# Attention scores in seven runs of three and two key blocks instead of eight of two, beside an MLP on one Trainium2 core

## The chip, the cores and the metric

The kernel runs on one core of one Trainium2 chip. Times are microseconds of the device for one execution. Before the change three runs gave a median of 1385.5 us (1382.28 to 1387.74). The core has a matrix engine (PE, with PEld for its weight loads), a vector engine (DVE), a scalar engine for activations (ACT), a general engine (POOL), and an engine that issues DMAs (SP). PE writes its results to PSUM, a small memory that DVE and ACT read; everything else lies in SBUF or in DRAM.

## The reference

For an input x of 2048 tokens by 640, with 32 heads of 20:

```python
xn = _layernorm(x, axis=-1)
# attention on xn
q, k, v = split(xn @ wqkv)                    # 32 heads of 20
scores = einsum("bhqd,bhkd->bhqk", q, k) * (Dh ** -0.5)
p = _softmax(scores, axis=-1)
A = merge(einsum("bhqk,bhkd->bhqd", p, v)) @ wo
# MLP on the normed xn, normed again
h = _gelu(_layernorm(xn) @ w1 + b1)           # 640 -> 1536
B = h @ w2 + b2                               # 1536 -> 640
return x + A + B
```

All is float32. The kernel computes the matrix products from pairs of float16 (a high and a low part) in three passes, and the product of exponentials and values partly in that way and partly in float32.

## The kernel before, in words

**Ahead of attention** (to about 232 us) the input is normed, transposed and projected to q, k and v. q, k and the normed input go to DRAM (`qkscr`, `xscr`), the factor of the second norm to `rscr`, and v stays in SBUF as `vfull`, with a column of ones a head.

**The attention stage** takes the heads in 16 pairs `g` and the queries in two halves `hf` of 1024, in the order `ORDER` (line 37). For each (g, hf) `load_stack` (line 131) brings a `qs` and a `ks`, each holding both heads of the pair with three stacked copies of 20 rows and a row for the shift, 61 rows a head. Each half has two columns of 512 queries, `cc`. For each of these 64 (g, hf, cc) there are 16 blocks `kb` of 128 keys; the texts call them a sixteen.

One block: `scores` (line 578) takes a buffer `s` of PSUM (pool `psS`, three buffers, line 53) and a buffer `p` of SBUF (pool `pt`, 2 * GRP - 1 = 7 buffers, line 517), issues two matmuls, one for each head (line 584, on the upper and the lower half of the PE's rows), and has ACT write the exponential to `p` (line 586). For blocks 0 and 1 of each four (`SPLIT`, line 25) `rest` (line 593) has DVE make `low`, what is left of `p` beyond its upper 16 bits (line 598; four buffers). `pv` (line 603) issues the products with the values for four blocks at once: eight matmuls with the upper halves, four with the `low`s, and for the two unsplit blocks four in float32, which show as eight records, all at line 615, into one PSUM buffer `o` (`psO`, one buffer). After a sixteen's last products ACT copies `o` to `ev` (line 636). `ev` holds both columns, and after the second one `unload` (line 644) issues six DMAs to `lpart` and `opart`, on SP, or on ACT for the last pair (`dma`, line 640). When a unit of heads is complete, `finish` (line 666) reads these back, divides and writes `oscr`.

**The MLP** is a generator, `mlp` (line 829), that yields the estimated cost of each step it has issued: 0.3276 for three matmuls of layer 1 (line 787), 0.272 for two of layer 2 (line 819). It takes 256 tokens a round, eight rounds. In layer 1 a unit is 30 matmuls into the one buffer of `psM`, and its last step begins `gelu` (line 735): DVE work at once, more at the next `tick`, tanh on ACT (line 748) two ticks later, the rest one tick later. In layer 2 a unit is 36 matmuls for 320 columns of 128 tokens, with `addup` behind it. Six units of layer 1 and four of layer 2 alternate in a round. `load_chunk` (line 769) loads a round's input `xm` and its factors `r2f` two rounds ahead. After the MLP `projection` (line 872) multiplies `oscr` with wo (line 896) and writes the output; it runs almost wholly behind attention.

**The order of the work** is written out by hand under `tc.manual_schedule()` (lines 927 to 983): each engine works through its instructions in the order in which they are issued here, and waits for semaphores. Before the change a group of four blocks is: two blocks' scores, a `tick` (which moves every open generator in `sides` one step), `rest` of the first, an MLP part; two more blocks' scores, a `tick`, `rest` of the others, and `pv` of the four blocks before. A part takes steps from the generator while `credit` is above zero, less than `CHUNK` has been spent, and no unit has ended (`over`); credit grows by `rate` at each part and is kept.

Of the kernel before, what the change touches and what calls it, by code (L numbers as in the profile page):

```python
# [7 lines left out]
F32 = mybir.dt.float32  # L8
# [8 lines left out]
P = 128  # L17
# [25 lines left out]
def mha_mlp_kernel(tc, x, wqkv, wo, w1, b1, w2, b2, out):  # L43
# [4 lines left out]
    with (  # L48
# [463 lines left out]
        with ExitStack() as scope:  # L512
# [1 line left out]
            m0 = pool(name="m0", bufs=2)  # L514
            m1 = pool(name="m1", bufs=1)
            m2 = pool(name="m2", bufs=2)
            ptp = pool(name="pt", bufs=2 * GRP - 1)


            sides = []  # L520
# [77 lines left out]
                    nc.vector.tensor_sub(low, pt, upper(pt))  # L598
                    unit.append(low)

            evs = {}

            def pv(units):

                g, hf, cc, kb0 = units[0][:4]
                if kb0 == 0:
                    pv.o = psO.tile([P, 512], F32, tag="o", name="o")  # L610
                    pv.begun = set()
                last = units[-1][3] == NKB - 1

                def product(q, src, v0, t):
                    nc.tensor.matmul(pv.o[32 * q : 32 * q + 32, :], src[:, v0 - PAD * (1 - q % 2) :][:, :32], t,  # L615
                                     start=q not in pv.begun, stop=last, skip_group_check=True)
                    pv.begun.add(q)

                split = [(u[3], upper(u[4]), u[5]) for u in units if SPLIT[u[3]]]
                whole = [(u[3], u[4]) for u in units if not SPLIT[u[3]]]  # L620
                of16 = lambda kb, a: 2 * PAD + kb * 2 * VROW + (2 * g + a) * 2 * VW
                of32 = lambda kb, a: PAD + kb * VROW + (2 * g + a) * VW
                for kb, up, _ in split:
                    for a in range(2):
                        product(2 * a, vhalf, of16(kb, a), up[:, a])
                        product(2 * a + 1, vhalf, of16(kb, a) + VW, up[:, a])
                for a in range(2):
                    for n, (kb, _, low) in enumerate(split):
                        product(2 * a + n % 2, vhalf, of16(kb, a), low[:, a])
                for a in range(2):  # L630
                    for n, (kb, pt) in enumerate(whole):
                        product(2 * a + n % 2, vfull, of32(kb, a), pt[:, a])
                if last:
                    if cc == 0:
                        evs[g, hf] = m1.tile([P, 2, 512], F32, tag="ev", name="ev")
                    nc.scalar.activation(evs[g, hf][:, cc], pv.o, AF.Copy)  # L636
                    if cc == 1:
                        unload(g, hf, evs.pop((g, hf)))

            def dma(g, hf):  # L640

                return (nc.scalar if (g, hf) == ORDER[-1] else nc.sync).dma_start

            def unload(g, hf, ev):
                cols = slice(hf * 1024, (hf + 1) * 1024)
                for p in range(2):
                    dma(g, hf)(lpart[p, hf, 2 * g : 2 * g + 2, :].rearrange("a (c t) -> a c t", c=2),
                                      ev[PAD + DH + VW * p :: 64])
                    for a in range(2):
                        q0, r = 64 * a + PAD + VW * p, (2 * g + a) * DH  # L650
                        dma(g, hf)(opart[p, r : r + DH, cols].rearrange("d (c t) -> d c t", c=2),
                                          ev[q0 : q0 + DH])
# [82 lines left out]
            def gelu(ps, r2f, hT, f):  # L735
                u = m1.tile([P, 2, MC], F32, tag="u", name="u")
                w = m1.tile([P, 2, MC], F32, tag="w", name="w")
                if f == 0:
                    nc.vector.tensor_scalar(r2f, r2f, f1, None, ALU.mult)
                nc.vector.tensor_mul(u, ps, r2f[:, None, :].to_broadcast([P, 2, MC]))  # L740
                nc.vector.tensor_add(u, u, b1t[:, f : f + 2, None].to_broadcast([P, 2, MC]))  # L741
                yield

                nc.vector.tensor_mul(w, u, u)  # L744
                nc.vector.scalar_tensor_tensor(w, w, 1.0 / 0.044715, u, ALU.add, ALU.mult)  # L745
                yield
                yield
                nc.scalar.activation(w, w, AF.Tanh, scale=0.7978845608028654 * 0.044715)
# [14 lines left out]

            NMC = S // MC

            xs, hTs = {}, {}
            over = [False]

            def load_chunk(mc):
                t0 = mc * MC  # L770
                xnt = m2.tile([P, KD, 2, MC], F16, tag="xnt", name="xm")
                r2f = m2.tile([P, MC], F32, tag="r2f", name="r2f")
                nc.sync.dma_start(xnt, xscr[:, :, :, t0 : t0 + MC])
                nc.sync.dma_start(r2f, rscr[None, t0 : t0 + MC].to_broadcast([P, MC]))
                xs[mc] = xnt, r2f

            def layer1(mc, f):
                xnt, r2f = xs[mc]
                if f == 0:
                    hTs[mc] = m0.tile([P, KF, 2, MC], F16, tag="hT", name="hT")  # L780
                ps = psM.tile([P, 2, MC], F32, tag="m", name="pu")
                for i in range(2):
                    n = 0
                    fo_ = (f + i) % 4 * P
                    for k in range(KD):
                        for a, b in PASS:
                            nc.tensor.matmul(ps[:, i], w1v[:, k, (f + i) // 4, a, fo_ : fo_ + P], xnt[:, k, b, :],  # L787
                                             start=(n == 0), stop=(n == 3 * KD - 1))
                            n += 1
                            if n % 3 == 0:  # L790
                                if i == 1 and n == 15:
                                    begin(gelu(ps, r2f, hTs[mc], f))
# [35 lines left out]

            def mlp():
                load_chunk(0)  # L830
                load_chunk(1)
                yield 2.0
                for mc in range(NMC + 1):
# [93 lines left out]
            with tc.manual_schedule():  # L927
                fill = chain()
                credit = 0.0 - next(fill)
                rate = 1.235  # L930
                groups = [(g, hf, cc, kb) for g, hf in ORDER for cc in range(2) for kb in range(0, NKB, GRP)]
                prev = None
                for g, hf, cc, kb0 in groups:
                    units = []
                    for kb in range(kb0, kb0 + GRP):
                        units.append([g, hf, cc, kb, scores(g, hf, cc, kb)])
                        if kb % 2 == 0:
                            continue
                        tick()
                        if kb % GRP == 1:  # L940

                            rest(units[0])
                            credit += rate
                            spent, over[0] = 0.0, False
                            while credit > 0 and spent < CHUNK and not over[0]:
                                cost = next(fill)
                                if cost is None:
                                    credit = 0.0  # L950
                                    break
                                credit -= cost
                                spent += cost
                        else:
                            for u in units[1:]:
                                rest(u)
                            if prev:
                                pv(prev)
                    prev = units
                    if cc == 0 and kb0 == 0 and (g, hf) != ORDER[-1]:  # L960
                        n = ORDER[ORDER.index((g, hf)) + 1]
                        sides.append(load_stack(*n, *([stacks[g, hf][1]] if n[0] == g else [])))
                n = 0
                ended[0] = True

# [9 lines left out]
                    return True  # L975

                more(2)
                pv(prev)
                while more(1):
                    pass  # L980
                while sides:
# [101 lines left out]
```

## Time and profile before

| | |
|---|---|
| median of three runs | 1385.5 us |
| the profiled execution's own time | 1385.2 us |
| its span | 1383.5 us |
| granted PE clock, mean | 0.997 |
| PE, DVE, ACT busy | 1350.8, 1061.7, 1126.2 us |
| first exponential of attention begins | 233.18 us |
| last products of attention begin | 1307.89 us |

A page row of a group names line, engine, operation, tiles and shapes and a count, then busy time and the mean of one in ns, then the idle time of the engine just before these instructions and what ended most of it. Rows in order of time begin with the start and the duration in us; a bracket names idle time before the first of them. Matmuls are pipelined and their ends are modelled, so the distance between two starts tells more than a duration.

### The profile page before, as it was taken

What the parts mean: (1) busy time and instruction counts of PE and PEld (TensorE: products, weight loads), DVE (VectorE), ACT (ScalarE), POOL (GpSimd) and SP (SyncE); (2) the same over time, 40 slices, a digit from 0 to 9 for tenths busy, and PEclk for the clock granted to TensorE, in tenths of its full rate; (3) what the DMA queues carried; (4) which work ended last, traced back from release to release, by engine and by line L of the source; (5) the groups of instructions that cost most, each with busy time, mean ns of one, the idle gap of its engine ahead of it and who ended that gap; (6) DMA issues with size and microseconds to landing.
All of it is one profiled execution on the core that took longest, in us unless ns stands there. A gap on an engine that the chain in (4) does not pass through costs nothing.

```text
span 1383.5 us, 29113 instructions
## 1 busy us (share of the span) xinstructions
PE 1350.8 (98%) x11711; PEld 600.9 (43%) x11711; DVE 1061.7 (77%) x1425; ACT 1126.2 (81%) x1282; POOL 32.9 (2%) x75
## 2 busy tenths in 40 slices
PE   9999999999999999999999999999999999999998
PEld 6555555443333343433343333343334334333375
DVE  6648743899778977889887789877988897888642
ACT  5644323999999999999999999999999999999700
POOL 2000000000000000000000000000000000000000
PEclk9999999999999999999999999999999999999999
DMA  9853413012124231213221123212124322341375
GB/s 265 243 175 109 108 52 110 16 32 64 41 55 111 67 88 34 69 52 102 71 77 33 47 75 103 76 47 58 44 64 113 98 56 70 85 153 59 98 235 179
DMA packets 92320, 125.68 MB, mean 91 GB/s; under 512 B 16905, under 2 KB 58569, under 8 KB 92178
## 3 DMA queue, kind: packets, MB, share of 16 engines
q1 hardware_dynamic: 89218, 117.14, 28.3%
q0 software_dynamic: 2304, 5.24, 2.3%
q8 instruction: 94, 1.54, 0.5%
q10 hardware_dynamic: 656, 1.36, 0.3%
q14 instruction: 48, 0.39, 0.1%
HBM read 80.84 MB, written 42.86 MB: 89 GB/s over the span
## 4 chain that ended last, share of the span: by engine, by line
PE 59%; DVE 11%; ACT 5%; DMA 3%; issue 2%; SPq 1%; DVEq 0%; ACTq 0%
PE o L615 23%; PE s L584 14%; PE py L819 9%; PE pu L787 8%; DVE low L598 5%; PE z L896 5%; ACT p L586 4%; DMA oscr<-oa 1%; DVE u L740 1%; DMA oa<-opart 1%; DVE u L741 1%; DVE w L744 1%; DVE w L745 1%; DVE hT L752 1%; DVE u L750 1%
## 5 line engine op out<-in xcount | busy, mean ns | idle before, releaser
L586 ACT ACTIVATE p<-s 128x1024 f32<-128x1024 f32 x1024 | 973.6, 1042 | 52.4 <-PE s L584 46.2
L598 DVE TENSOR_TENSOR low<-p 128x1024 f16<-128x1024 f32 x512 | 608.8, 1219 | 165.0 <-ACT p L586 164.9
L615 PE MATMUL o<-p,vfull 128*32 128x512 bf16 (+1 forms) x4096 | 433.7, 494 | 0.0
L584 PE MATMUL s<-qs,ks 61*128 61x512 f16 x2048 | 317.7, 382 | 8.7 <-ACT p L586 7.2
L584 PEld LDWEIGHTS <-ks 61*128 61x128 f16 x2048 | 63.9, 94 | 296.4 <-issue 294.2
L787 PE MATMUL pu<-xm,w1t 128*128 128x256 f16 x1440 | 179.2, 274 | 4.1 <-DVE u L740 3.6
L819 PE MATMUL py<-w2t,hT 128*128 128x320 f16 x1152 | 178.6, 301 | 1.7 <-DVE xb L757 1.7
L787 PEld LDWEIGHTS <-w1t 128*128 128x128 f16 x1440 | 130.9, 98 | 71.2 <-issue 57.6
L819 PEld LDWEIGHTS <-hT 128*128 128x128 f16 x1152 | 102.5, 98 | 89.5 <-issue 55.2
L286 PE MATMUL qkp<-xnt,wv 128*128 128x512 f16 x600 | 132.3, 380 | 0.0
L615 PEld LDWEIGHTS <-vfull 128*32 128x32 f16 x3072 | 61.5, 95 | 146.2 <-issue 115.4
L615 PE MATMUL o<-low,vfull 128*32 128x512 f16 x1024 | 107.3, 379 | 6.6 <-DVE low L598 6.4
L300 ACT ACTIVATE qkhl<-qkp,qks 128x1024 f16<-128x1024 f32 (+1 forms) x24 | 23.3, 971 | 84.1 <-PE qkp L286 66.2
L286 PEld LDWEIGHTS <-wv 128*128 128x128 f16 x600 | 58.2, 98 | 67.8
L615 PEld LDWEIGHTS o<-p,vfull 128*32 128x32 f32 x2048 | 63.1, 109 | 50.6 <-issue 0.5
L349 PE MATMUL vp<-wv,xnt 128*128 128x320 f16 x480 | 66.6, 300 | 0.0
L896 PE MATMUL z<-w1t,ot 128*128 128x320 f16 x480 | 65.8, 300 | 0.0
L896 PEld LDWEIGHTS <-ot 128*128 128x128 f16 x480 | 46.7, 98 | 19.8 <-issue 1.7
L349 PEld LDWEIGHTS <-xnt 128*128 128x128 f16 x480 | 46.5, 98 | 18.2
L301 DVE SCALAR_TENSOR_TENSOR qkhl<-qkp,qks,qkhl 128x1024 f16<-128x1024 f32 (+1 forms) x24 | 26.5, 1104 | 34.3 <-ACT qkhl L300 34.3
L857 DVE SCALAR_TENSOR_TENSOR acc<-z,sc,acc 128x320 f32<-128x320 f32 x32 | 17.6, 550 | 45.1 <-PE z L896 42.9
L636 ACT ACTIVATE ev<-o 128x512 f32<-128x512 f32 x64 | 39.4, 615 | 3.3 <-PE o L615 3.3
(168 smaller groups left out, 685.7 us busy)
## 6 DMA issues: line engine op xcount, KB each, us to landing
qkscr<-qkhl SPq DMA_DIRECT2D x40, 256.0 KB
opart<-ev SPq DMA_DIRECT2D x124, 80.0 KB
ks<-qkscr SPq DMA_DIRECT2D x120, 80.0 KB
qs<-qkscr SPq DMA_DIRECT2D x192, 40.0 KB
oa<-opart SPq DMA_DIRECT2D x32, 240.0 KB
xt<-in_A_x_dram SPq DMA_DIRECT2D x16, 320.0 KB
xscr<-xnt SPq DMA_DIRECT2D x4, 1280.0 KB
xm<-xscr SPq DMA_DIRECT2D x8, 640.0 KB
```

Source lines behind the costliest of these rows:

```text
L286: nc.tensor.matmul(ps[:, i, :], wv[:, k, q, a, mm * P : (mm + 1) * P], xnts[c][:, k, b, :], start=(k + n == 0), stop=(k == KD - 1 and n == 2))
L300: nc.scalar.activation(hl[:, 0, i0:i1], ps[:, i0:i1], AF.Copy, scale=a)
L301: nc.vector.scalar_tensor_tensor(hl[:, 1, i0:i1], ps[:, i0:i1], a, hl[:, 0, i0:i1], ALU.mult, ALU.subtract)
L349: nc.tensor.matmul(ps[:, hf, :320], xnts[c][:, k, a, j * P : (j + 1) * P], wv[:, k, 2, b, hf * 320 : (hf + 1) * 320], start=(n == 0), stop ...
L584: nc.tensor.matmul(ps[:, a, :], ks[64 * a : 64 * a + 61, kb * P : (kb + 1) * P], qs[64 * a : 64 * a + 61, cc * 512 : (cc + 1) * 512], star ...
L586: nc.scalar.activation(pt, ps, AF.Exp, scale=QS)
L598: nc.vector.tensor_sub(low, pt, upper(pt))
L615: nc.tensor.matmul(pv.o[32 * q : 32 * q + 32, :], src[:, v0 - PAD * (1 - q % 2) :][:, :32], t, start=q not in pv.begun, stop=last, skip_gr ...
L636: nc.scalar.activation(evs[g, hf][:, cc], pv.o, AF.Copy)
L787: nc.tensor.matmul(ps[:, i], w1v[:, k, (f + i) // 4, a, fo_ : fo_ + P], xnt[:, k, b, :], start=(n == 0), stop=(n == 3 * KD - 1))
L819: nc.tensor.matmul(ps[:, :320], hTs[mc][:, f, a, j * P : (j + 1) * P], w2v[:, f, b, hf * 320 : (hf + 1) * 320], start=(n == 0), stop=(n == ...
L896: nc.tensor.matmul(ps[:, :320], ot[:, k, a, j * P : (j + 1) * P], wov[:, k, b, h * 320 : (h + 1) * 320], start=(n == 0), stop=(n == 3 * KD ...
```

## The change

- The order: a sixteen's scores go in seven runs, ending after blocks 3, 5, 7, 9, 12, 14 and 16 (so 3, 2, 2, 2, 3, 2, 2 blocks). Behind the runs stand, in this order: an MLP part, the products of the last four blocks of the sixteen before, an MLP part, the products of blocks 0 to 3, those of 4 to 7, an MLP part, those of 8 to 11. `rest` follows each run for all its blocks. There are seven ticks for eight.
- MLP parts: three for four; `rate` 1.647 for 1.235, `CHUNK` 2.0 for 1.75.
- Buffers: eight of exponentials for seven. `ev` holds one column, and is unloaded after each. `r2f` has one buffer for two and is loaded by itself, one round ahead, where the last unit of layer 1 has begun its GELU.
- `gelu` has one tick fewer ahead of tanh.

```diff
-CHUNK = 1.75
+CHUNK = 2.0
...
-            ptp = pool(name="pt", bufs=2 * GRP - 1)
+            ptp = pool(name="pt", bufs=2 * GRP)
...
                 if last:
-                    if cc == 0:
-                        evs[g, hf] = m1.tile([P, 2, 512], F32, tag="ev", name="ev")
-                    nc.scalar.activation(evs[g, hf][:, cc], pv.o, AF.Copy)
-                    if cc == 1:
-                        unload(g, hf, evs.pop((g, hf)))
+                    ev = m1.tile([P, 512], F32, tag="ev", name="ev")
+                    nc.scalar.activation(ev, pv.o, AF.Copy)
+                    unload(g, hf, cc, ev)
...
-            def unload(g, hf, ev):
-                cols = slice(hf * 1024, (hf + 1) * 1024)
+            def unload(g, hf, cc, ev):
+                c0 = cc * 512
                 for p in range(2):
-                    dma(g, hf)(lpart[p, hf, 2 * g : 2 * g + 2, :].rearrange("a (c t) -> a c t", c=2),
-                                      ev[PAD + DH + VW * p :: 64])
+                    dma(g, hf)(lpart[p, hf, 2 * g : 2 * g + 2, c0 : c0 + 512], ev[PAD + DH + VW * p :: 64])
                     for a in range(2):
                         q0, r = 64 * a + PAD + VW * p, (2 * g + a) * DH
-                        dma(g, hf)(opart[p, r : r + DH, cols].rearrange("d (c t) -> d c t", c=2),
-                                          ev[q0 : q0 + DH])
-                if g + 1 in ENDS:
+                        dma(g, hf)(opart[p, r : r + DH, hf * 1024 + c0 : hf * 1024 + c0 + 512], ev[q0 : q0 + DH])
+                if cc == 1 and g + 1 in ENDS:
...
                 yield
-                yield
                 nc.scalar.activation(w, w, AF.Tanh, scale=0.7978845608028654 * 0.044715)
...
+            def load_factors(mc):
+                r2f = m1.tile([P, MC], F32, tag="r2f", name="r2f")
+                nc.sync.dma_start(r2f, rscr[None, mc * MC : (mc + 1) * MC].to_broadcast([P, MC]))
+                fs[mc] = r2f
...
                 if f == KF - 2:
+                    if mc + 1 < NMC:
+                        load_factors(mc + 1)
                     if mc + 2 < NMC:
                         load_chunk(mc + 2)
...
-                rate = 1.235
-                groups = [(g, hf, cc, kb) for g, hf in ORDER for cc in range(2) for kb in range(0, NKB, GRP)]
...
+                rate = 1.647
+                after = {3: "mlp", 5: -GRP, 7: "mlp", 9: 0, 12: GRP, 14: "mlp", 16: 2 * GRP}
+                prev, units, new = None, [], []
+                for g, hf in ORDER:
+                    for cc in range(2):
+                        prev, units = units, []
+                        for kb in range(NKB):
+                            units.append([g, hf, cc, kb, scores(g, hf, cc, kb)])
+                            new.append(units[-1])
+                            work = after.get(kb + 1)
+                            if work is None:
+                                continue
+                            tick()
+                            for u in new:
                                 rest(u)
+                            new.clear()
+                            if work == "mlp":
...
+                            elif work >= 0:
+                                pv(units[work : work + GRP])
+                                units[work : work + GRP] = [None] * GRP
+                            elif prev:
+                                pv(prev[work:])
+                                prev = None
+                                del u
...
                 more(2)
-                pv(prev)
+                pv(units[-GRP:])
```

More of the change, by code (lines that the diff above doesn't have):

```diff
@@ new lines, in mha_mlp_kernel @@
+                rate = 1.647
[12 more added lines that the diff above has]
+                            for u in new:
+                                rest(u)
+                            new.clear()
+                            if work == "mlp":
+                                credit += rate
+                                spent, over[0] = 0.0, False
+                                while credit > 0 and spent < CHUNK and not over[0]:
+                                    cost = next(fill)
+                                    if cost is None:
+                                        credit = 0.0
+                                        break
+                                    credit -= cost
+                                    spent += cost
+                            elif work >= 0:
[5 more added lines that the diff above has]
+                                del u
+                            if cc == 0 and work == -GRP and (g, hf) != ORDER[-1]:
+                                n = ORDER[ORDER.index((g, hf)) + 1]
+                                sides.append(load_stack(*n, *([stacks[g, hf][1]] if n[0] == g else [])))
```

39 lines of the change are left out of this document (5 added, 34 removed).

## The prediction

> **What bounds the kernel now.** I read the page first, then the groups by line, then the waits, then the order of time of a few stretches, because the change moves instructions within one stage.
>
> ```profile
> span 1383.5 us, 29113 instructions
> PE 1350.8 (98%) x11711; PEld 600.9 (43%) x11711; DVE 1061.7 (77%) x1425; ACT 1126.2 (81%) x1282; POOL 32.9 (2%) x75
> PE   9999999999999999999999999999999999999998
> ACT  5644323999999999999999999999999999999700
> L586 ACT ACTIVATE p<-s 128x1024 f32<-128x1024 f32 x1024 | 973.6, 1042 | 52.4 <-PE s L584 46.2
> L584 PE MATMUL s<-qs,ks 61*128 61x512 f16 x2048 | 317.7, 382 | 8.7 <-ACT p L586 7.2
> PE s L584 <- ACT p L586: 7.2, 24, 0.5
> PE o L615 <- DVE low L598: 6.4, 11, 1.5
> 700.00:800.00 100.00, 98.75 (x931) 39.21 (x929) 80.72 (x88) 96.38 (x109) 0.87 (x1) 1.00 0.18 45
> ```
>
> The slices show two nearly full engines from slice 8 to slice 37: that is the attention stage, and in the window 700 to 800 PE is busy 98.75 us and ACT 96.38 us, at a granted clock of 1.00. ACT's idle time before the exponentials (52.4 us) waits on PE's scores. PE itself waits little: 7.2 us in 24 waits for an exponential, 6.4 us in 11 waits for a `low`. So PE's stream of instructions sets the time, with ACT close behind. The time to sum against is the profiled execution's 1385.2 us (its span is 1383.5); the median of the three runs is 1385.5, so both bases are the same within 0.3 us.
>
> **The prices.** One stretch of the order of time gives them all, as distances between starts on PE and on ACT.
>
> ```profile
> 702.22 1.16 PE L787 MATMUL pu<-xm,w1t 128*128 128x256 f16 x9
> 703.31 0.61 PE L584 MATMUL s<-qs,ks 61*128 61x512 f16 x4
> 703.84 0.64 PE L615 MATMUL o<-p,vfull 128*32 128x512 bf16 x8
> 705.49 0.61 PE L584 MATMUL s<-qs,ks 61*128 61x512 f16 x4
> 705.77 0.63 ACT L636 ACTIVATE ev<-o 128x512 f32<-128x512 f32 x1
> 706.03 1.81 PE L787 MATMUL pu<-xm,w1t 128*128 128x256 f16 x15
> 706.25 3.96 ACT L586 ACTIVATE p<-s 128x1024 f32<-128x1024 f32 x4
> 707.78 0.61 PE L584 MATMUL s<-qs,ks 61*128 61x512 f16 x4
> 710.09 0.63 ACT L748 ACTIVATE w<-w 128x512 f32<-128x512 f32 x1
> 710.61 9.52 ACT L586 ACTIVATE p<-s 128x1024 f32<-128x1024 f32 x10
> ...
> 727.15 1.25 PE L819 MATMUL py<-w2t,hT 128*128 128x320 f16 x8
> 728.33 0.61 PE L584 MATMUL s<-qs,ks 61*128 61x512 f16 x4
> 731.65 0.61 PE L584 MATMUL s<-qs,ks 61*128 61x512 f16 x4
> 732.08 4.00 ACT L586 ACTIVATE p<-s 128x1024 f32<-128x1024 f32 x4 [0.64 <-PE s L584]
> 732.19 1.53 PE L819 MATMUL py<-w2t,hT 128*128 128x320 f16 x10
> 733.65 0.60 PE L584 MATMUL s<-qs,ks 61*128 61x512 f16 x4
> ```
>
> ```profile
> 233.18 7.44 ACT L586 ACTIVATE p<-s 128x1024 f32<-128x1024 f32 x8
> 234.25 0.39 PE L584 MATMUL s<-qs,ks 61*128 61x512 f16 x2 [0.52 <-ACT p L586]
> 272.73 0.39 PE L584 MATMUL s<-qs,ks 61*128 61x512 f16 x2 [0.19 <-ACT p L586]
> 273.05 0.66 PE L615 MATMUL o<-p,vfull 128*32 128x512 bf16 x8
> ...
> 349.78 1.03 ACT L586 ACTIVATE p<-s 128x1024 f32<-128x1024 f32 x1 [0.38 <-PE s L584]
> ```
>
> ```profile
> L748 ACT ACTIVATE w<-w 128x512 f32<-128x512 f32 x48 | 30.6, 637 | 0.0
> ```
>
> A run of two blocks (four matmuls) takes 703.84 - 703.31 = 0.53, and one block that began alone behind a wait 273.05 - 272.73 = 0.32. So a block is **0.21** and every run carries **0.11** on top. Four blocks of products are 705.49 - 703.84 = **1.65**. An MLP part of 9 matmuls is 1.09 and one of 15 is 1.75: **0.11 a matmul and 0.11 a part**; in layer 2, 8 take 1.18 and 10 take 1.46, or 0.135 each and 0.12 a part. On ACT, eight exponentials run in 7.44, one alone shows 1.03, so they follow each other by (7.44 - 1.03) / 7 = **0.915**; `ev` delays the next by 0.48, tanh by 0.52. An exponential starts **0.45** behind the start of its block (732.08 - 731.65 = 0.43, rounded up for others at 0.49). A score buffer is free for PE **1.07** after its exponential began (234.25 - 233.18).
>
> For 16 blocks of keys, PE needs 8 x 0.53 + 4 x 1.65 + 4.94 of MLP (the rate, 4 x 1.235) + 4 x 0.11 = 16.2, ACT 16 x 0.915 + 0.48 + 0.75 x 0.52 = 15.5 (48 tanh, L748's row, on 64 sixteens). ACT has 0.7 to spare on the average, and only three score buffers to carry it over PE's other work.
>
> **What goes.** Seven runs for eight and three parts for four: two pieces fewer in each of 64 sixteens, 2 x 0.11 x 64 = **-13.9 us**. Products and MLP matmuls are as many as before.
>
> [...]
>
> The waits of the products for a `low` go too. They came because block 1's `low` (of each four) was issued on DVE behind a whole MLP part's GELU work, with its products one run away. Now the `low`s of a run follow that run, and their products stand four blocks or more later. A record's end is modelled 0.38 after its start while starts lie 0.21 apart, so each recorded wait hides another 0.17: 6.4 + 11 x 0.17 = **-8.3 us** (bounds: 0, if as many remain, and -8.3).
>
> **What comes: waits for score buffers.** Block n writes the buffer of block n-3, so it waits for that exponential. Before, with runs of two and X between them, the second block reuses the first block's buffer of the last run: free at 0.45 + 1.07 = 1.52 from that run's start, reached at 0.53 + X + 0.21. X may be as short as 0.78; products (1.65) leave 0.87 to spare. With a run of three this changes:
> - Two, products, three: the third block needs the second's buffer, free at 0.45 + 0.915 + 1.07 = 2.43, reached at 0.53 + 1.65 + 0.42 = 2.60. Spare: 0.17, for blocks 2 and 11 of each 16.
> - Three, X, two: again 2.43, reached at 0.74 + X + 0.21. X must be 1.48: products leave 0.17, an MLP part of 9 matmuls (1.09) is 0.39 short, one of 4 (0.66) is 0.82 short.
>
> Any backlog on ACT adds: `ev`, tanh, a score left over. And the parts get unequal. A part ends at 2.0 us of credit or at a unit's end; layer 1's unit (30 matmuls) falls into 21 + 9 and layer 2's (36) into 16 + 16 + 4, as the built order shows, where before most parts were 8 to 12. ACT starves behind the long ones (2.4 and 2.3 us) and PE stands behind the short ones.
>
> I carried these prices through the built order of both kernels, block by block (PE in its order; a block not before 1.07 after the start of exponential n-3; ACT in its order). From first to last block before comes to 1048.0 with 16.1 of such waits. The trace has 1304.78 - 232.47 = 1072.3 there:
>
> ```profile
> 232.47 0.61 PE L584 MATMUL s<-qs,ks 61*128 61x512 f16 x4
> 1304.78 0.61 PE L584 MATMUL s<-qs,ks 61*128 61x512 f16 x4
> ```
>
> The rest is waits for DVE and DMA, which I left out, and a slower start. After comes to 1059.0 with 44.3 of waits (block 4: 12.3, block 2: 10.6, block 11: 7.5, block 15: 7.4), and 3.5 us of matmuls (20 of layer 2, 6 of the projection) now stand behind the last score, moved and not added. The waits grow by **+28.2 us**. Bounds: before, the trace records 24 waits, 7.2 + 24 x 0.17 = 11.3, where the same walk has 15.3 in waits longer than 0.17; scaled by that 0.74 the growth is +20.9. With 0.943 between exponentials, (9.52 - 1.03) / 9 from the row of ten at 710.61, in which short waits are merged, the walk gives +35. I take 28, the plain price.
>
> **Unloading and the rest.** `ev` is unloaded after each half, so 192 more DMA issues, all but the last pair's on SP, at about half a microsecond by the rows below. SP waits for ACT there (370.6 us in 22 waits), so it is early; what stands behind a waiting unload are loads of stacks needed eight or more blocks later: nothing. `ev` has one buffer, written every 16 us, and its six issues take 3.2 us (below), so it is free long before: nothing. For the last pair the issues are ACT's own, and the new set comes in the middle of its exponentials:
>
> ```profile
> SPq L647 <- ACT ev L636: 370.6, 22, 29.9
> 1310.31 1.08 ACTq L647 DMA_DIRECT2D lpart<-ev  x1
> 1311.42 0.72 ACTq L651 DMA_DIRECT2D opart<-ev  x2
> 1312.17 0.50 ACTq L647 DMA_DIRECT2D lpart<-ev  x1
> 1312.71 0.86 ACTq L651 DMA_DIRECT2D opart<-ev  x2
> ```
>
> That is 1.08 + 0.72 + 0.50 + 0.86 = 3.2 us in which PE runs out of score buffers; less the spare in them, **+2 us** (bounds 0 and 3.2).
>
> The eighth buffer of exponentials keeps the old rule (the ninth block's exponential needs a buffer whose first products follow its score at once), GELU's missing step brings tanh one run earlier (L748 waits 0.0 us now), and r2f's load comes two parts ahead of its use. Each costs nothing while ACT's 0.7 us a sixteen covers it; a tanh late by 0.7 in half of 48 cases would be 17 us of ACT, most of it in that slack.
>
> **Sum:** 1385.2 - 13.9 - 8.3 + 28.2 + 2 = 1393.2.
>
> **The rivals.**
> - *Forecast, 1393 (0.58):* pieces saved, more given back at the score buffers. For it: PE's small spare is arithmetic on recorded starts. Its own range, 1387 to 1399, comes from the bounds above.
> - *The buffers hold (0.14): faster, 1377.* PE and ACT settle into a rhythm where a wait at one block spares the next, and the added waits are half of 28, none on ACT at the end: 1385.2 - 13.9 - 8.3 + 14 = 1377.0. It decides from the point where the added waits fall below 22. For it: the walk overstates before's waits by a quarter. Against: parts of 4 and 9 matmuls stand behind a run of three in 3 of 8 sixteens, whatever the rhythm.
> - *ACT becomes the bound (0.18): 1404.* With the late tanh and 0.943 between exponentials, waits grow by 35, the `low` waits stay half: 1385.2 - 13.9 - 4 + 35 + 3 = 1405. For it: ACT at 96.38 of 100. [...]
> - *Nothing to see (0.10): 1386.* Waits by the lower bound (+20.9) cancel the two gains: 1385.2 - 13.9 - 8.3 + 20.9 + 2 = 1385.9.
>
> **How the numbers follow.** A measurement of this kernel can tell about 0.5% (6.9 us) from no change, so slower begins at 1392.4. The forecast's range lies on both sides of it: 0.34 slower, 0.24 the same. With the rivals: faster 0.13 (the first rival, with 0.01 of it the same), same 0.35, slower 0.52. The range 1377 to 1405 takes in both bounds of the waits.
>
> **What would show it.** In the profile of the changed kernel: runs of six score matmuls; L584's wait for exponentials up from 7.2 to 20 or 30 us, in some 100 waits, at the third block of a run and behind short parts; the products' wait for `low` near zero; one gap of 2 us on PE in the last sixteen. If that wait stays under 15 us the time falls below before's; if ACT waits for DVE at tanh, or PE for a DMA, I have missed a cost.

## The result, and the profile after

The changed kernel takes a median of 1389.54 us (1388.3 to 1391.44, nine runs), the kernel before 1385.48 us (1382.28 to 1387.74, nine runs): a ratio of 1.0026 [1.0018, 1.0035]. It is slower, by about 4 us; forecast were 1393 us, 8 us more than before. The profiled execution took 1390.37 us.

The first fence is the page of the changed kernel, with the rows that answer to those shown of before (line 613 was 615, 783 was 787, 817 was 819). A row's columns are as before: busy time and mean in ns, then idle time ahead and what ended it.

```profile
span 1388.7 us, 29501 instructions
PE 1346.0 (97%) x11711; PEld 623.0 (45%) x11711; DVE 1065.4 (77%) x1425; ACT 1120.0 (81%) x1282; POOL 33.5 (2%) x75
PE   8999999999999999999999999999999999998898
ACT  5644323999999999999999999999999999999500
L586 ACT ACTIVATE p<-s 128x1024 f32<-128x1024 f32 x1024 | 969.9, 1053 | 55.0 <-PE s L584 50.9 <-DVE w1t L556 3.3
L584 PE MATMUL s<-qs,ks 61*128 61x512 f16 x2048 | 320.4, 382 | 27.9 <-ACT p L586 25.0 <-ACT vfull L359 0.3
L783 PE MATMUL pu<-xm,w1t 128*128 128x256 f16 x1440 | 175.2, 274 | 1.9 <-DVE u L734 1.8
L817 PE MATMUL py<-w2t,hT 128*128 128x320 f16 x1152 | 173.1, 300 | 0.1
L613 PE MATMUL o<-low,vfull 128*32 128x512 f16 x1024 | 100.3, 379 | 0.0
```

And the two waits of PE and ACT that matter, in the view of waits (total us, times, longest us), still of the changed kernel:

```profile
PE s L584 <- ACT p L586: 25.0, 82, 3.6
ACT p L586 <- PE s L584: 50.9, 137, 1.2
```

Both engines are as full as before and PE has 4.8 us less recorded work (1346.0 for 1350.8: fewer pieces, and a modelled sum, so only a direction). What grew is one wait: PE's for an exponential that still reads the score buffer it needs, 25.0 us in 82 waits for 7.2 in 24. The products' wait for a `low` is 0.0 (6.4 before). The row of slices has two 8s near its end and one at its start, where there were 9s.

Where the time went can be read from the first and the last block of scores (before's rows, 232.47 and 1304.78, stand in the prediction):

```profile
233.28 0.61 PE L584 MATMUL s<-qs,ks 61*128 61x512 f16 x4
1307.11 0.61 PE L584 MATMUL s<-qs,ks 61*128 61x512 f16 x4
```

Between them lie 1073.8 us, 1.5 more than before (1072.3). Behind the last one come 81.6 us to the end of the span for 78.7, which is 2.9 more, near the 3.5 us of matmuls that the prediction moved there. The stretch ahead took 0.8 longer. So in the attention stage the saving and the waits nearly cancel.

The order of time shows the mechanism. Columns: start, duration, engine and line, what; a bracket is idle time ahead.

```profile
722.33 2.45 PE L783 MATMUL pu<-xm,w1t 128*128 128x256 f16 x21
724.72 0.60 PE L584 MATMUL s<-qs,ks 61*128 61x512 f16 x4
...
726.90 0.82 PE L584 MATMUL s<-qs,ks 61*128 61x512 f16 x6
727.65 0.65 PE L613 MATMUL o<-p,vfull 128*32 128x512 bf16 x8
...
729.84 1.16 PE L783 MATMUL pu<-xm,w1t 128*128 128x256 f16 x9
730.93 0.68 PE L584 MATMUL s<-qs,ks 61*128 61x512 f16 x4
...
733.18 0.60 PE L584 MATMUL s<-qs,ks 61*128 61x512 f16 x4
733.96 0.39 PE L584 MATMUL s<-qs,ks 61*128 61x512 f16 x2 [0.17 <-ACT p L586]
734.29 2.35 PE L817 MATMUL py<-w2t,hT 128*128 128x320 f16 x16
736.57 0.61 PE L584 MATMUL s<-qs,ks 61*128 61x512 f16 x4
...
1296.46 0.81 ACTq L646 DMA_DIRECT2D opart<-ev  x2
1297.38 3.77 ACT L586 ACTIVATE p<-s 128x1024 f32<-128x1024 f32 x4 [3.34 <-DVE w1t L556]
1298.45 0.61 PE L584 MATMUL s<-qs,ks 61*128 61x512 f16 x2 [3.58 <-ACT p L586]
1298.99 1.05 PE L613 MATMUL o<-p,vfull 128*32 128x512 bf16 x8
...
1301.90 0.82 PE L584 MATMUL s<-qs,ks 61*128 61x512 f16 x6
```

A run of three, six matmuls, lasts 727.65 - 726.90 = 0.75. The MLP's parts are 21 and 9 matmuls in layer 1 and 16 in layer 2: a part of 21 holds PE for 724.72 - 722.33 = 2.39 us, one of 9 for 1.09. At 733.96 the third block of a run of three, behind products, waits for its buffer: the place where the arithmetic left 0.17 to spare. Counted along this order, 37 of the 82 waits (6.8 us) stand at that place, 22 (11.2 us, with the one of 3.58) behind an MLP part of 4 matmuls and 15 (2.8 us) behind one of 9. At the end is the other thing: the six unload issues of the last pair stand on ACT's queue, ACT's exponentials stand behind them for 3.34 us (the releaser named, `w1t`, is not what held them: the rows just above are ACT's own queue), and PE for 3.58.

### The profile page after: what moved, and what is told of

Read it like the earlier page. It is cut to its first block, busy times and chain, and to the rows that moved or that the text cites. A ratio compares the mean times of both kernels' runs of the same rounds, so it can differ in the third digit from the quotient of the medians.

```text
span 1388.7 us, 29501 instructions
## 1 busy us (share of the span) xinstructions
PE 1346.0 (97%) x11711; PEld 623.0 (45%) x11711; DVE 1065.4 (77%) x1425; ACT 1120.0 (81%) x1282; POOL 33.5 (2%) x75
## 4 chain that ended last, share of the span: by engine, by line
PE 73%; ACT 12%; issue 6%; DVE 5%; DMA 3%; ACTq 0%; SPq 0%; POOL 0%; DVEq 0%
PE o L613 21%; PE s L584 15%; ACT p L586 11%; PE py L817 10%; PE pu L783 9%; PE qkp L286 7%; PE z L895 5%; PE vp L349 4%; DVE low L598 2%; DMA qkscr<-qkhl 1%; DMA w1t<-in_A_wo_dram 1%; PE pt L262 1%; DMA xt<-in_A_x_dram 0%; DMA oa<-opart 0%; DVE wv L383 0%
## 5 line engine op out<-in xcount | busy, mean ns | idle before, releaser
L586 ACT ACTIVATE p<-s 128x1024 f32<-128x1024 f32 x1024 | 969.9, 1053 | 55.0 <-PE s L584 50.9
L584 PE MATMUL s<-qs,ks 61*128 61x512 f16 x2048 | 320.4, 382 | 27.9 <-ACT p L586 25.0
L584 PEld LDWEIGHTS <-ks 61*128 61x128 f16 x2048 | 82.7, 94 | 337.8 <-issue 319.8
L783 PE MATMUL pu<-xm,w1t 128*128 128x256 f16 x1440 | 175.2, 274 | 1.9 <-DVE u L734 1.8
L817 PE MATMUL py<-w2t,hT 128*128 128x320 f16 x1152 | 173.1, 300 | 0.1
L783 PEld LDWEIGHTS <-w1t 128*128 128x128 f16 x1440 | 133.8, 98 | 52.8 <-issue 38.1
L613 PEld LDWEIGHTS <-vfull 128*32 128x32 f16 x3072 | 58.6, 95 | 117.4 <-issue 87.0
L613 PE MATMUL o<-low,vfull 128*32 128x512 f16 x1024 | 100.3, 379 | 0.0
L301 DVE SCALAR_TENSOR_TENSOR qkhl<-qkp,qks,qkhl 128x1024 f16<-128x1024 f32 (+1 forms) x24 | 26.5, 1105 | 35.0 <-ACT qkhl L300 35.0
```

The lines of the kernel that those rows point to most:

```text
L301: nc.vector.scalar_tensor_tensor(hl[:, 1, i0:i1], ps[:, i0:i1], a, hl[:, 0, i0:i1], ALU.mult, ALU.subtract)
L584: nc.tensor.matmul(ps[:, a, :], ks[64 * a : 64 * a + 61, kb * P : (kb + 1) * P], qs[64 * a : 64 * a + 61, cc * 512 : (cc + 1) * 512], star ...
L586: nc.scalar.activation(pt, ps, AF.Exp, scale=QS)
L817: nc.tensor.matmul(ps[:, :320], hTs[mc][:, f, a, j * P : (j + 1) * P], w2v[:, f, b, hf * 320 : (hf + 1) * 320], start=(n == 0), stop=(n == ...
```

## The experiments

Theory A: the six unload issues on ACT cost more than the 2 us given to them. Theory B: most of the other waits come from the unequal MLP parts, not from the run of three as such. The rivals are beside each. All ratios are to the kernel before, run on the same chip, with 95% intervals; the medians of the kernel before on the three chips of the experiments are 1385.26, 1386.15 and 1386.86 us, a microsecond or so apart. Differences below are of medians, good to about that; whether there is a difference is read from the intervals.

| kernel | median us | ratio to before | PE's wait for exponentials, us in times |
|---|---|---|---|
| changed kernel | 1389.54 | 1.0026 [1.0018, 1.0035] | 25.0 in 82 |
| first unload of the last pair on SP | 1384.64 | 0.9988 [0.9973, 1.0002] | 21.3 in 82 |
| even MLP parts | 1365.60 | 0.9842 [0.9810, 0.9874] | 10.2 in 16 |
| both | 1365.37 | 0.9838 [0.9799, 0.9877] | 7.2 in 17 |
| both, other order of seven runs | 1363.50 | 0.9832 [0.9809, 0.9856] | 5.6 in 9 |
| even parts in layer 1 alone | 1380.37 | 0.9967 [0.9949, 0.9986] | 21.4 in 58 |
| seven buffers of exponentials | 1411.19 | 1.0185 [1.0157, 1.0214] | 39.9 in 133 |
| GELU's step back | 1393.94 | 1.0067 [1.0045, 1.0089] | 26.5 in 89 |
| eight runs, the rest of the change | 1409.99 | 1.0156 [1.0123, 1.0190] | 13.1 in 31 |
| the same, second `low` behind the MLP part | 1396.49 | 1.0072 [1.0048, 1.0096] | 9.5 in 22 |
| the same, and first unload on SP | 1391.27 | 1.0031 [1.0020, 1.0042] | 6.5 in 21 |
| the same, and GELU's step back | 1387.74 | 1.0002 [0.9990, 1.0013] | 7.1 in 23 |

### The last pair's unload

The first half's `ev` of the last pair is unloaded by SP; the second half's stays on ACT.

```diff
-            def dma(g, hf):
+            def dma(g, hf, cc=1):
...
-                return (nc.scalar if (g, hf) == ORDER[-1] else nc.sync).dma_start
+                return (nc.scalar if (g, hf) == ORDER[-1] and cc else nc.sync).dma_start
```

with `dma(g, hf, cc)` in `unload`.

> The changed kernel, with the last pair's first unload issued by SP and not by ACT. Theory A (ACT's six issues stand among the last sixteen's exponentials: PE waited 3.58 us there, and the 33 instructions behind the gap took some 1.3 us longer than elsewhere): the wait of 3.58 us is gone, 4 to 6 us faster than the changed kernel, about 1384.5. Rival (the gap would be there anyway, because ACT is behind at that point): no more than 1 us.

Measured: 1384.64 us, ratio 0.9988 [0.9973, 1.0002], 4.9 us less than the changed kernel by the medians (0.38% or 5.3 us by the ratios). The view of waits, and the same place in the order of time (columns as above):

```profile
PE s L584 <- ACT p L586: 21.3, 82, 0.5
```

```profile
1291.48 0.60 ACT L633 ACTIVATE ev<-o 128x512 f32<-128x512 f32 x1
1291.98 2.86 ACT L586 ACTIVATE p<-s 128x1024 f32<-128x1024 f32 x3
```

The exponentials follow `ev` at once, with no idle time in a bracket, and PE's longest wait falls from 3.6 to 0.5; the number of waits stays 82. Only the one gap went, and with it about 5 us. That is more than the gap's 3.58, for what follows the gap was slow too: in the changed kernel 1301.90 - 1298.45 = 3.45 us pass for one block and four blocks' products, which elsewhere take 0.32 + 1.65 = 1.97. The windows (length, then busy time and count of PE, PEld, DVE, ACT and POOL, then the granted clock, DMA share, GB/s) of the changed kernel say why:

```profile
1200.00:1290.00 90.00, 85.15 (x785) 34.79 (x774) 72.23 (x99) 84.77 (x101) 1.98 (x2) 1.00 0.34 101
1298.00:1303.00 5.00, 4.55 (x36) 1.21 (x39) 4.06 (x7) 3.82 (x5) 0.00 (x0) 0.66 0.00 1
1303.00:1310.00 7.00, 7.00 (x72) 2.80 (x64) 4.40 (x6) 5.96 (x7) 1.59 (x2) 1.00 0.01 2
```

The granted clock is 1.00 before, 0.66 in the five microseconds behind the gap and 1.00 after them. So the price of the issues is the gap, 3.6, and the slow stretch, 3.45 - 1.97 = 1.5: together 5.1 beside 4.9 measured. A shorter gap did the same: in the kernel with even parts (below), a gap of 2.74 us at this place is followed by a clock of 0.50, which sets in about 1 us behind it:

```profile
1273.00:1274.00 1.00, 0.85 (x14) 0.38 (x17) 0.98 (x2) 1.00 (x3) 0.00 (x0) 1.00 0.00 0
1274.40:1277.40 3.00, 3.00 (x18) 0.31 (x13) 2.49 (x6) 2.22 (x3) 0.00 (x0) 0.50 0.00 0
```

So in these runs PE was slowed behind a gap of 2.74 us as it was behind 3.58.

### The MLP's parts, made even

One number: a part of the MLP ends at 1.6 of credit spent. A unit of layer 1 then falls into 15 + 15 matmuls and one of layer 2 into 12 + 12 + 12: as many parts as 21 + 9 and 16 + 16 + 4, only evenly cut.

```diff
-CHUNK = 2.0
+CHUNK = 1.6
```

> The changed kernel with CHUNK at 1.6 in place of 2.0, so that layer 1's unit of 30 matmuls falls into 15 + 15 (not 21 + 9) and layer 2's of 36 into 12 + 12 + 12 (not 16 + 16 + 4): as many parts and pieces as in the changed kernel. Theory B (PE's added waits for score buffers come from the short parts, 1.09 and 0.66 us against the 1.48 needed behind a run of three, and ACT starves behind the long ones): PE's wait at L584 for exponentials falls from 25.0 us in 82 waits to under 10, ACT's wait for scores from 50.9 to under 35, and the time to 1355 to 1368. Rival (the run of three itself makes the waits, by the spare of only 0.17 behind products): the wait stays above 18 us and the time above 1383. Rival (a piece costs less than 0.11, so seven runs never brought 13.9 us): the wait falls, but the time stays above 1375.

Measured: 1365.60 us, ratio 0.9842 [0.981, 0.9874]: 24 us below the changed kernel, 20 below before (22 by the ratio). The waits and one stretch of PE's order:

```profile
PE s L584 <- ACT p L586: 10.2, 16, 2.7
ACT p L586 <- PE s L584: 22.2, 112, 0.8
```

```profile
717.11 1.81 PE L783 MATMUL pu<-xm,w1t 128*128 128x256 f16 x15
718.85 0.61 PE L584 MATMUL s<-qs,ks 61*128 61x512 f16 x4
...
721.03 0.82 PE L584 MATMUL s<-qs,ks 61*128 61x512 f16 x6
721.79 1.80 PE L817 MATMUL py<-w2t,hT 128*128 128x320 f16 x12
723.52 0.61 PE L584 MATMUL s<-qs,ks 61*128 61x512 f16 x4
```

Both kinds of part now last the same: 718.85 - 717.11 = 1.74 and 723.52 - 721.79 = 1.73, more than the 1.48 that the two behind a run of three needs, and that two starts at 723.52 without a bracket. The wait, at 10.2 us, is just above the 10 expected, 2.74 of it at the last pair. It falls by 14.8 us and 66 times; with 0.17 hidden in each (the prediction's estimate) that is 14.8 + 66 x 0.17 = 26.0, beside a gain of 24. The waits behind parts of 4 and 9 are gone with those parts, and those at the third block behind products fall from 37 to 7, though the runs of three stand as before: most of them were a backlog that the unequal parts had made. ACT's wait for scores falls too, from 50.9 to 22.2. That the long parts had starved it, and left it no slack for the short ones, fits this but was not tried by itself. The two windows 700 to 800, the changed kernel's and then this one's, show the rate:

```profile
700.00:800.00 100.00, 98.42 (x926) 42.31 (x926) 81.84 (x90) 94.93 (x108) 1.72 (x2) 1.00 0.20 54
```

```profile
700.00:800.00 100.00, 99.67 (x942) 42.42 (x938) 80.49 (x86) 97.98 (x111) 0.87 (x1) 1.00 0.18 49
```

In the same 100 us PE does 942 matmuls for 926 and ACT is busy 97.98 us for 94.93. Theory B holds: with runs of three in place, cutting the same filler evenly takes away most of the waits. The rival that a piece costs less than 0.11 had the time stay above 1375, and it did not.

### Even parts in one layer, in both with the unload, and in another order

Three variations. First, the smaller cut in layer 1 alone (layer 2 stays 16 + 16 + 4):

```diff
-                                spent, over[0] = 0.0, False
-                                while credit > 0 and spent < CHUNK and not over[0]:
+                                spent, over[0], cap = 0.0, False, CHUNK
+                                while credit > 0 and spent < cap and not over[0]:
...
+                                    cap = 1.6 if cost > 0.3 else CHUNK
```

> The changed kernel with layer 1's parts even (15 + 15) and layer 2's as they are (16 + 16 + 4). Theory B (short parts make the waits, each by what it is short of 1.48 us): the parts of 9 are gone and those of 4 remain, so the time falls about half way, 1375 to 1383, and PE's wait for exponentials is 12 to 20 us (25.0 in the changed kernel, 10.2 with all parts even). Rival (only the parts of 4 matter, 0.82 short against 0.39): above 1385.

Measured: 1380.37 us, 0.9967 [0.9949, 0.9986], 9 us below the changed kernel; PE's wait 21.4 us in 58, above the 12 to 20 expected, though the time is as expected. ACT's wait for scores falls to 37.0. The 15 waits behind parts of 9 are gone, those at the third block fall from 37 to 28, and the 22 behind parts of 4 stay, with 11.2 us as before. So layer 1's cut is worth less than half of the 24 us; by subtraction the rest belongs to layer 2, whose part of 4 was the shortest, though layer 2's cut was not tried alone.

Second, both edits so far together:

> Both edits of e1 and e2. If they are apart from each other, the gains add: 4 to 6 us below e2, 1350 to 1363. If the gap at the end is made by ACT being behind, even parts take it away too, and this equals e2 within 1 us.

Measured: 1365.37 us, 0.9838 [0.9799, 0.9877], which cannot be told from even parts alone. The profile shows the gap gone (wait 7.2 in 17, longest 1.2, for 10.2 in 16, longest 2.7), but the two gains do not add up clearly. With even parts the gap at the last pair was 2.74 us and not 3.58, with a slow stretch of 1.5 us behind it as well (the block, the four blocks' products and the run of three behind the gap take 1277.38 - 1273.15 = 4.23 for 0.32 + 1.65 + 0.75), so about 4.2 us were to be won. The rows of the last scores and of the projection behind them, first of even parts alone, then of both, show where some of it went:

```profile
1281.38 0.60 PE L584 MATMUL s<-qs,ks 61*128 61x512 f16 x4
1316.25 3.98 PE L895 MATMUL z<-w1t,ot 128*128 128x320 f16 x28 [0.24 <-DMA ot<-oscr]
```

```profile
1276.90 0.60 PE L584 MATMUL s<-qs,ks 61*128 61x512 f16 x4
1314.38 5.88 PE L895 MATMUL z<-w1t,ot 128*128 128x320 f16 x42 [0.91 <-DMA ot<-oscr]
```

The last scores begin 4.5 us sooner, the projection's last long part only 1.9: behind attention PE now waits for the read-back of the last heads. These are single executions; how much the medians hide stays open.

Third, on top of both, the order 2, 2, 3, 2, 2, 3, 2:

```diff
-                after = {3: "mlp", 5: -GRP, 7: "mlp", 9: 0, 12: GRP, 14: "mlp", 16: 2 * GRP}
+                after = {2: "mlp", 4: -GRP, 7: "mlp", 9: 0, 11: "mlp", 14: GRP, 16: 2 * GRP}
```

> The kernel of e3 with another order in a sixteen: runs of 2, 2, 3, 2, 2, 3, 2 blocks with an MLP part behind blocks 2, 7 and 11 and products behind 4, 9, 14 and 16. Now a run of three never stands behind products and ahead of products with a run of two behind it. Theory (what is left of PE's wait in e3, 7.2 us recorded, comes at the third block behind products, with 0.17 to spare): 1 to 5 us faster than e3. Rival (the rest of e3's loss is not there): the same as e3, 1361 to 1367.

Measured: 1363.50 us, 0.9832 [0.9809, 0.9856], with 5.6 us of waits in 9. The waits at the third block behind products fall from 8 to 2, as expected, but another one of 3.0 us appears. It has the lowest median of all, but lies within the interval of the order as changed.

### The eighth buffer of exponentials

```diff
-            ptp = pool(name="pt", bufs=2 * GRP)
+            ptp = pool(name="pt", bufs=2 * GRP - 1)
```

> The changed kernel with seven buffers of exponentials, as before the change. Theory (the seven-run order needs the eighth: block 7's exponential would have to wait for the products of blocks 0 to 3, which stand behind block 8's score on PE): ACT waits for products, PE then for ACT, 10 to 30 us slower than the changed kernel. Rival (the buffer keeps the old rule and buys nothing): within 3 us of it.

Measured: 1411.19 us, 1.0185 [1.0157, 1.0214]: 22 us above the changed kernel. The waits of this kernel:

```profile
ACT p L586 <- PE o L613: 49.7, 75, 1.4
PE s L584 <- ACT p L586: 39.9, 133, 4.0
```

A new line: ACT waits 49.7 us for products that have not yet read the buffer it is to write, and PE then waits more often for ACT (133 times for 82). With eight buffers there is no such wait in the changed kernel. So the new order cannot do with the seven buffers of before; the eighth is a part of the price of the order.

### Eight runs with all the rest of the change

The rest alone: runs of two and four MLP parts as before, with eight buffers, `ev` by columns, `r2f` by itself, GELU's step out, and `rest` behind each run for all its blocks.

```diff
-CHUNK = 2.0
+CHUNK = 1.75
...
-                rate = 1.647
+                rate = 1.235
...
-                after = {3: "mlp", 5: -GRP, 7: "mlp", 9: 0, 12: GRP, 14: "mlp", 16: 2 * GRP}
+                after = {2: "mlp", 4: -GRP, 6: "mlp", 8: 0, 10: "mlp", 12: GRP, 14: "mlp", 16: 2 * GRP}
```

> All of the change but its order: eight runs of two, four MLP parts at the rate and CHUNK of before, with the changed kernel's buffers (eight exponentials, ev by columns, one r2f), its GELU with one step fewer and both lows behind their run. Theory (the change lost by its order of parts, and the rest is nothing or a small loss): between 1385 and 1398, with the wait for exponentials near before's 7.2 us and the MLP's waits for DVE higher than before's 5.3 us, as GELU's steps now stand before the lows. Rival (the buffers alone are a gain that the order loses again): below 1382.

Measured: 1409.99 us, 1.0156 [1.0123, 1.019]. That was missed by far: the rest of the change, without its order, costs more than the whole. The groups and the waits of this kernel:

```profile
L783 PE MATMUL pu<-xm,w1t 128*128 128x256 f16 x1440 | 180.5, 275 | 17.9 <-DVE u L734 12.5 <-DVE xb L750 3.9 <-DMA xm<-xscr 0.6
L817 PE MATMUL py<-w2t,hT 128*128 128x320 f16 x1152 | 179.4, 301 | 11.8 <-DVE u L734 7.3 <-DVE xb L750 4.4
```

```profile
ACT w L741 <- DVE w L739: 30.8, 38, 3.2
```

Here it is the MLP that waits, for DVE (17.9 + 11.8 us), and ACT for DVE's part ahead of tanh (30.8 us). Both `low`s of a run now stand on DVE ahead of the GELU work of the part behind that run. The next kernel puts the second `low` behind the MLP part again, as in the kernel before:

```diff
-                            for u in new:
+                            n_ = 1 if work == "mlp" else len(new)
+                            for u in new[:n_]:
                                 rest(u)
-                            new.clear()
+                            del new[:n_]
```

> The kernel of e5 (eight runs of two, all of the change but its order), with one thing as before the change: in front of an MLP part only the first block's low is issued, and the second one's behind the part's GELU. Theory (e5 lost 25 us because both lows stand ahead of GELU on DVE, where the second waits for its exponential and holds up the instruction that frees the MLP's one PSUM buffer): PE's and ACT's waits for GELU's DVE work (u and w: 12.5 + 7.3 and 30.8 us in e5) fall under 8 in all, products wait for a low again (5 to 10 us), and the time is 1383 to 1391. Rival (the missing GELU step, the columns of ev or r2f made it): it stays above 1400.

Measured: 1396.49 us, 1.0072 [1.0048, 1.0096]. The waits went the way that was expected, though not quite as far: those for `u` fall to 2.2 us and that ahead of tanh to 7.3 (9.5 in all, for under 8), and the products' wait for `low` comes back (11.4 us in 20, for 5 to 10). The time came out between the theory (1383 to 1391) and its rival (above 1400): about 10 us above before were still unexplained. Two kernels took them apart, first the unload as above, then GELU's step too:

> The kernel of e6 (eight runs, one low ahead of each MLP part, the change's buffers and its GELU with one step fewer), with the last pair's first unload issued by SP. It should lose what e1 lost: if ACT's issues cost 5 us in this order too, 1391 to 1392; if they are hidden behind the eight runs' larger spare, 1395 to 1397.

> The kernel of e9 with GELU's step put back: before the change, but for eight buffers of exponentials, ev by columns with twice the DMAs, and one r2f. Theory (the missing step sets GELU's work on DVE ahead of a low that products wait for, 11.4 us in 20 waits in e6 against 6.4 in 11 before): equal to before within 3 us, 1383 to 1388. Rival (the buffers and the many small unloads cost by themselves): 1389 or more.

Measured: 1.0031 [1.002, 1.0042] and 1.0002 [0.999, 1.0013]. So the issues on ACT cost 5.2 us in this order too (1396.49 - 1391.27), and GELU's missing step 3.5 us (1391.27 - 1387.74). With the step back the products' waits for a `low` fall from 10.6 us in 20 to 6.7 in 12, as its theory had it. What is then left of the change, eight buffers, `ev` and its unloads by columns on SP and `r2f` by itself, costs nothing that can be measured.

### GELU's step in the seven-run order

```diff
                 yield
+                yield
                 nc.scalar.activation(w, w, AF.Tanh, scale=0.7978845608028654 * 0.044715)
```

> The changed kernel with GELU's step put back, so that tanh comes two runs behind the part as before. Theory (in the order of seven runs no products wait for a low, so the step is free either way): within 2 us of the changed kernel, 1387.5 to 1391.5. Rival (the missing step costs ACT, which waits 4.4 us at tanh for DVE): 3 to 6 us faster.

Measured: 1393.94 us, 1.0067 [1.0045, 1.0089], about 4 us above the changed kernel; neither theory had that. PE's wait for exponentials is 26.5 us in 89 (25.0 in 82), ACT's for scores 57.7 in 164 (50.9 in 137), and ACT's 4.4 us of waits for DVE ahead of tanh are gone. PE's waits thus grow by 1.5 + 7 x 0.17 = 2.7 us, as much as the time from the first to the last block of scores (1076.5 for 1073.8). So in this order the step's absence is worth having, and in the eight-run order it costs. That a later tanh falls upon ACT at a worse place among the exponentials is an argument, not shown; the cause stays open.

## Why the prediction was right or wrong

**Right in direction and mechanism.** The score buffers give back more than the saved pieces bring. L584's wait went to 25.0 us, within the 20 to 30 named, in 82 waits instead of some 100; 74 of them stand at the two places named, 37 at the third block of a run behind products and 37 behind short parts. Evening out the parts showed that their inequality makes most of both. The products' waits for `low` went wholly, the -8.3 of the sum. A run of three takes 0.75 for the 0.74 worked out.

**The size was off: +4 measured, +8 forecast.** The step that failed is the term for the score buffers, taken 4.3 us too high; next to it, a cost of the MLP was left out whose fall is worth almost as much (3.8). Two errors the other way, some 3 us at the last pair and about 1 in the pieces, made up for half of this: that the sum came no further off is luck. Term by term:

- *Score buffers, +28.2.* Without the end gap the trace has 25.0 - 3.58 = 21.4 us in 81 waits, 21.4 + 81 x 0.17 = 35.2 with the hidden parts, against 11.3 before: **+23.9**. The walk's plain price was 4.3 too high; the truth lay between it and the lower bound of 20.9. This was the largest error: the bound scaled by the trace of before (7.2 us in 24 waits, where the walk had more) was the nearer row. Why the walk makes too many waits stays open. The 0.17 hidden in each is an estimate, but without it the even parts (26.0 for 24 us) and layer 1's alone (below) would not come out.
- *The last pair's issues, +2 (0 to 3.2).* **About +5**, outside the bounds. By the sum, none of the issues was covered: PE's gap is 3.58 us for 3.1 us of issues and the 0.48 of `ev` ahead of them. The slow stretch behind the gap was not in the sum at all.
- *MLP behind DVE, not in the sum.* Before, the MLP's matmuls waited 4.1 + 1.7 = 5.8 us ahead of their records, after 1.9 + 0.1 = 2.0. The rows of before:

```profile
L787 PE MATMUL pu<-xm,w1t 128*128 128x256 f16 x1440 | 179.2, 274 | 4.1 <-DVE u L740 3.6
L819 PE MATMUL py<-w2t,hT 128*128 128x320 f16 x1152 | 178.6, 301 | 1.7 <-DVE xb L757 1.7
```

  That is **-3.8**, which I left out because I followed DVE only where the products waited for it.
- *Pieces, -13.9.* By its own factors, 2 x 0.11 x 64, this is 14.1. Not measured by itself. With the other four terms, -8.3 + 23.9 + 5 - 3.8 = +16.8, the measured +4.1 leaves -12.7 for it (with the errors of the other four in it), in keeping with 0.11 a piece (-13.9).
- *"Each costs nothing".* True of `r2f` and the unloads on SP (eight runs with both: 1.0002). Not true of GELU's step, which is worth about 4 us, of one sign in eight runs and of the other in seven. The eighth buffer costs nothing either, and is needed, as the prediction had it: without it 22 us are lost. The sign that was named for a missed cost did come, ACT waiting for DVE at tanh (4.4 us), but with the step back that wait is gone and the time is longer, so the missed cost was not there.

**The rivals.** *Nothing to see* (1386) was as near in time as the forecast, 3.6 us below for 3.7 above: its waits by the lower bound, +20.9, are 3 us below those found, and its 2 us for the end were 3 short. *The buffers hold* needed added waits under 22; they were 23.9 in the changed kernel. *ACT becomes the bound* (1404 by its name, 1405 by its sum) did not come: ACT waits 50.9 us for scores, no less than before (46.2).

**Where the expected gain went.** By the balance above the saving is real, and it was given back at a place that the order of runs does not fix: the unequal parts that `CHUNK` = 2.0 cuts. With 1.6 the same order is 1.6% faster than before (1365.6 us); with the unload moved 1365.4, and with the other order of runs 1363.5. These three beat both kernels and cannot be told from each other.

## What to carry to other kernels

When one engine's work is the filler between bursts that use few PSUM buffers, look at the shortest and the longest piece of filler, not at the mean: the same number of pieces, evenly cut, was worth 24 us of 1390 here, six times what the whole change moved. Count a DMA issued on the queue of an engine that sets the pace as that engine's time: the six here took 3.1 us of ACT, and where PE then stood still for 3.58 us at the last pair (2.74 with even parts), its granted clock behind the gap was 0.54 (0.50). When several edits come together, run the rest without the main one: here a step of GELU that had been called free was worth about 4 us, with a sign that depended on the order, and the place of one `low` 13.5 us (1409.99 - 1396.49).

## What the runs showed of the hardware

- Behind the gap of 3.58 us on PE, the granted clock was 0.66 over 1298 to 1303 and 1.00 over 1303 to 1310; the eight records of bf16 products took 1.05 us for 0.65 elsewhere (at 727.65). The slow stretch cost 1.5 us more than the wait that the view of waits counts.
- Behind a gap of 2.74 us it was 0.50 (even parts, 1274.4 to 1277.4), beside 0.54 behind the 3.58 (changed kernel, 1298.45 to 1301.9), but 1.00 behind one of 2.66 us in the other order of seven runs (1273.4 to 1278).
- Six DMA issues took 3.1 us of ACT (1.08 + 0.72 + 0.50 + 0.81), for 3.2 in the kernel before, where they stood behind the last exponentials. The rows of the changed kernel:

```profile
1294.07 1.08 ACTq L643 DMA_DIRECT2D lpart<-ev  x1
1295.17 0.72 ACTq L646 DMA_DIRECT2D opart<-ev  x2
1295.93 0.50 ACTq L643 DMA_DIRECT2D lpart<-ev  x1
1296.46 0.81 ACTq L646 DMA_DIRECT2D opart<-ev  x2
```
- The total of a recorded wait can be a poor measure of a cost: with layer 1's parts even, PE's wait for exponentials fell only from 25.0 to 21.4 us, and the time by 9. The 24 waits fewer, at 0.17 hidden in each, make it 3.6 + 24 x 0.17 = 7.7.
